# Bias of two chunks in one load, and the order of the first loads: fused attention and MLP on one core

## The chip, the cores and the metric

The kernel runs on one core of a Trainium2 chip. The metric is the device time of one execution in microseconds (us), the median of three runs. KB are 1024 bytes. The core has five engines with a queue of instructions each: TensorE (PE, with its weight loads as PEld), VectorE (DVE), ScalarE (ACT), GpSimd (POOL) and SyncE (SP). SP issues nearly all DMAs of this kernel, in the order of its queue; 16 DMA engines carry them.

## What is computed

Attention with a bias that depends on the distance of two positions, then an MLP over the result (batch 4, 8 heads, 576 positions, head dimension 64):

```python
scores = scale * np.matmul(q, k.transpose(0, 1, 3, 2))
psi_rel = np.log1p(np.abs(rel))
x = (psi_rel / psi_i)[..., None]
h = np.maximum(x @ w1 + b1, 0.0)
bias = h @ w2
scores = scores + bias.transpose(2, 0, 1)[None, :, :, :]
attn = np.exp(scores - max); attn = attn / attn.sum()
out = np.matmul(attn, v)
# then, on x = out as (batch, 576, 512)
u = x + (xt @ U @ V).transpose(0, 2, 1)
result = u + np.maximum(u @ w_ch1, 0.0) @ w_ch2
```

The bias is the same for all four batches; it differs by head.

## The kernel before

**The bias table.** In the first 58 us the kernel computes the bias of all heads, 16 positions at a time (36 blocks), and writes each block to a table in DRAM (`bias_dram`, stored by `bias_out`, L308). From there it comes back as the scores need it. The last five stores of the table hold the last rows, which the last chunks read.

**Pairs, slots, chunks.** Heads are worked in pairs: 16 pairs p (4 batches of 4 head pairs). Only pairs 0 to 3 load bias; pairs 4 to 15 use the same four tiles `bias[hp]` again. The 576 query positions are four chunks c of 128 and a rest of 64 (called c = 4). A pair has nine slots s. Slot 0 works the rest of both heads, slot 1 + 2c the first head of chunk c, slot 2 + 2c its second head. So slots 5 and 6 use chunk 2, and slots 7 and 8 use chunk 3. In a slot (`scores`), TensorE computes a score block of 128x576 into one of two buffers in PSUM, VectorE adds the bias and takes the row minimum of the negated sum (`p<-sc,bias`, L366), ScalarE takes the exponent, and two slots later TensorE transposes the block. Slot 8 ends with a product with v (`av`, out `o`).

**The loads of bias.** `bias_loads(c, hp)` returns the loads of one chunk for one head pair, as closures. A chunk has three: the first head (128 rows of 576 numbers, 288 KB), and the second head in a long part of 512 columns (256 KB) and a short part of 64 columns (32 KB), as its columns stand in the tile in another order. The rest (c = 4) has two loads of 144 KB on 64 partitions each.

**The order of loads.** All of them are issued by SP. A list `loads` holds closures; each slot takes the first two (three in pair 0) and issues them. SP's queue runs ahead of the other engines: a DMA goes out when the ones before it in the queue have gone out and its own waits are over. Each DMA also takes one of eight counters in turn, and SP waits until the DMA that had this counter before has landed; so no more than eight are under way. In the rows of SP's order below these counters are the names DMAHW0 to DMAHW7. A load of bias that reads table rows just stored waits for those stores too.

**Other loads in the same queue.** `load_v` brings v of a pair (320 KB), `load_part` brings q and k of a pair into `raw` in four loads of 304 KB on 64 partitions each, from which GpSimd prepares `hi` and `lo` (`prep_ops`) for the pair after. From slot 0 of pair 2 on, weights of the MLP come too (`wraw`). After the pairs the MLP runs, with a dense TensorE to the end.

Around the change, `bias[p + 1]` of a later pair is asked for in two parts: the rest and chunks 0 and 1 at the pair's start, chunks 2 and 3 (`late`) at its slot 8.

Of the kernel before, what the change touches and what calls it, by code (L numbers as in the profile page):

```python
# [19 lines left out]
B, H, S, D = 4, 8, 576, 64  # L20
# [6 lines left out]
P = 128  # L27
HALF = S // 2
LEFT = S - 4 * P
K0 = 2 * S + LEFT  # L30
QKW = 2 * K0
# [28 lines left out]
def kernel(  # L60
# [14 lines left out]
    nc = tc.nc  # L75
# [52 lines left out]
    bias = {hp: big.tile([P, 9 * S], F32, tag=f"big{hp}", name=f"bias{hp}") for hp in range(2)}  # L128
# [20 lines left out]
    def load_part(p, a, e):  # L149
        b, hp = divmod(p, HP)  # L150
        for lo in (0, D):
            nc.sync.dma_start(out=raw[lo : lo + D, a:e], in_=qk[b, hp, :, a:e])

    def load_v(p):
        b, hp = divmod(p, HP)
        v_t[p] = vpp.tile([P, 640], F32, tag="v", name="v")
        nc.sync.dma_start(out=v_t[p], in_=vp[b, hp])
# [153 lines left out]

    def row(i, h, a, e):
        return bd[i, h * ROW + SHIFT + a : h * ROW + SHIFT + e]

    def bias_loads(c, hp):

        if c < 4:
            i = slice(c * P, (c + 1) * P)
            h, j = 2 * hp, (1 + 2 * c) * S
            parts = [  # L320
                (bias[hp][:, j : j + S], row(i, h, 0, S)),
                (bias[hp][:, j + S + LEFT : j + 2 * S], row(i, h + 1, 0, S - LEFT)),
                (bias[hp][:, j + S : j + S + LEFT], row(i, h + 1, S - LEFT, S)),
            ]
        else:
            i = slice(4 * P, S)
            parts = [(bias[hp][t * LEFT : (t + 1) * LEFT, 0:S], row(i, 2 * hp + t, 0, S)) for t in range(2)]
        return [lambda o=o, i=i: nc.sync.dma_start(out=o, in_=i) for o, i in parts]
# [417 lines left out]
    loads = []  # L746
# [4 lines left out]
    for i in range(len(order) + 2):  # L751
# [4 lines left out]
        if i == len(order) - 1:  # L756
            nc.gpsimd.tensor_scalar(
                out=warm, in0=hids[order[i]][3][:, 0:1], scalar1=1.0, scalar2=0.0, op0=ALU.mult, op1=ALU.add
# [17 lines left out]
    p0.close()  # L776
    psT2 = ctx.enter_context(tc.tile_pool(name="psT2", bufs=2, space=PSUM))
    rot = {"s": [psS], "t": [psT, psT2, psT2]}
    for c, hp in ((4, 1), (0, 1), (3, 0), (1, 1)):
        loads += bias_loads(c, hp)  # L780
    loads += [lambda: load_v(1)] + bias_loads(2, 1)
    loads += [lambda: load_part(2, 0, K0), lambda: load_part(2, K0, QKW)] + bias_loads(3, 1)


    nc.vector.tensor_tensor(out=fold, in0=ident[:, 0 : 2 * RANK], in1=ident[:, 2 * RANK : P], op=ALU.add)
# [1 line left out]
        out=rep[:, 0 : 3 * RANK].rearrange("p (g r) -> p g r", g=3),  # L787
# [5 lines left out]
        out=rep[:, 3 * RANK : P], in0=fold[:, 0:RANK], in1=fold[:, 0:RANK], op=ALU.subtract  # L793
# [28 lines left out]
    for p in range(NP):  # L822
        if p > 0:
            new_pair(p)
        if 0 < p < HP - 1:
            bias[p + 1] = big.tile([P, 9 * S], F32, tag=f"big{p + 1}", name=f"bias{p + 1}")
            loads += [o for c in (4, 0, 1) for o in bias_loads(c, p + 1)]
            late = [o for c in (2, 3) for o in bias_loads(c, p + 1)]
        for s in range(9):
            if s == (1 if p else 0) and p < NP - 1:  # L830
                prep = prep_ops(p + 1)
# [151 lines left out]
    for j in range(3, NB, 2):  # L983
        if j == 3:
            l = utp.tile([P, 4 * LINE + UT], F32R, tag="utl3", name="ut")[:, 4 * LINE :]
            h, l = h3, [(0, l3), (2, l.rearrange("p (k f) -> p k f", k=2))]
        else:
            h = utp.tile([P, KD, 2 * TB], F32R, tag=f"uth{j}", name="ut")
# [15 lines left out]
    def turns(j):  # L1004
        return [lambda a=a, i=i: make_ut(a, i) for a in (j, j + 1) for i in range(TT)] if j < NB else [lambda: None] * 4
# [62 lines left out]
    def store(q, which):  # L1068
        w, to = flat(q, which), (w1_dram, w2_dram)[which][q]
        parts = [slice(o, o + 2 * DM) for o in range(0, w.shape[1], 2 * DM)]  # L1070
        return [lambda c=c: nc.sync.dma_start(out=to[:, c], in_=w[:, c].bitcast(F32)) for c in parts]
# [88 lines left out]
    a = token_sums(5, ([acc[2], acc[3]], [acc[4], acc[5]], [acc[6], acc[7]], [acc[8], acc[9]]), False)  # L1160
# [13 lines left out]
    for u in [(0, j, h) for j in (3, 5, 7) for h in range(2)]:  # L1174
        todo = mlp1(u) + (mlp2(last) if last else [])
        a = turns(u[1] + 2)[2 * u[2] : 2 * u[2] + 2]
# [161 lines left out]
    for q in range(NQ):  # L1338
        final = q == NQ - 1
        new = (w1_sums(q) if q else []) + stream(jobs[q], jobs[q + 1][:2])  # L1340
        late = (store(q - 1, 1) if 0 < q <= 4 else []) + (store(q, 0) if q < 4 else [])
# [3 lines left out]
        segs, c = layer1(q)  # L1345
# [16 lines left out]
    for n, q in enumerate(order2):  # L1362
# [4 lines left out]
        one, c = layer1(q)  # L1367
# [84 lines left out]
```

## Time and profile before

| | us |
|---|---|
| median of three runs | 731.37 |
| lowest and highest run | 730.5, 731.55 |
| the profiled execution | 730.93 |
| its span, from the first to the last instruction | 729.2 |
| TensorE busy in it | 707.6 (97%) |
| VectorE, ScalarE, GpSimd busy | 534.0, 402.6, 265.0 |

The 1.7 us between the span and the execution's time lie around the program. The granted clock of TensorE is 1.00 of its higher level (2.4 GHz) over the whole span. In the rows, L366 is line 366 of the kernel, `out<-in` names tiles, and `<-` in brackets names what ended an engine's idle time.

### The profile page before, as it was taken

Reading aid. Unit: us, or ns where it says so; the run is one execution under the profiler, and the core shown is the slowest. Engines: PE = TensorE matmul, PEld = TensorE weight load, DVE = VectorE, ACT = ScalarE, POOL = GpSimd, SP = SyncE. Lnnn points to the kernel's source line nnn. Section 1 sums busy time; section 2 is a strip of 40 time slices with the busy share of each in tenths; the row PEclk is TensorE's granted clock in tenths of the full one; section 3 lists DMA queues with packets and bytes.
Section 4 is the critical chain, followed back from the end, with each engine's and each line's share of the span. In section 5 each row is a group of like instructions: output and inputs, shape, how many; then the busy total and the mean of one; then the engine's idle time right before and its main releaser. Section 6 shows DMA issues by size and latency. Waiting matters only on the chain.

```text
span 729.2 us, 13122 instructions
## 1 busy us (share of the span) xinstructions
PE 707.6 (97%) x4620; PEld 562.0 (77%) x4620; DVE 534.0 (73%) x1202; ACT 402.6 (55%) x915; POOL 265.0 (36%) x281
## 2 busy tenths in 40 slices
PE   6899999999999999999999999999999999999997
PEld 3446887788777777879787888888787788888886
DVE  7985577788888767665658779989999964655545
ACT  7896777788878768774223235555555421222220
POOL 0004666667756657801141332536346400000000
PEclk9999999999999999999999999999999999999999
DMA  6889997475556556632192613647434674633313
GB/s 195 274 308 311 266 262 197 124 201 144 160 156 174 126 133 174 179 120 87 66 345 107 236 35 119 226 148 262 158 130 159 228 263 168 259 123 129 159 58 116
DMA packets 53874, 129.06 MB, mean 177 GB/s; under 512 B 8881, under 2 KB 12465, under 8 KB 52529
## 3 DMA queue, kind: packets, MB, share of 16 engines
q1 hardware_dynamic: 53568, 127.97, 54.8%
q8 instruction: 37, 0.61, 0.4%
q14 instruction: 29, 0.23, 0.1%
q10 hardware_dynamic: 240, 0.26, 0.1%
HBM read 83.21 MB, written 44.99 MB: 176 GB/s over the span
## 4 chain that ended last, share of the span: by engine, by line
PE 68%; DVE 9%; ACT 8%; DMA 8%; POOL 3%; issue 3%; SPq 1%; POOLq 0%; DVEq 0%; ACTq 0%
PE po L1287 15%; PE sb L1226 12%; PE o L468 9%; PE sc L364 9%; PE tb L432 6%; PE ph L635 5%; PE po L660 4%; DMA bias<-bias_dram 3%; PE bs L291 3%; DMA raw<-in_qk_dram 2%; POOL wy L229 1%; PE ph L1315 1%; DMA u_dram<-acc 1%; DVE acc L1273 1%; ACT ring L271 1%
## 5 line engine op out<-in xcount | busy, mean ns | idle before, releaser
L1273 DVE TENSOR_TENSOR acc<-po,acc 128x512 f32<-128x512 f32 x108 | 74.0, 687 | 50.2 <-PE po L1287 42.8
L385 ACT ACTIVATE p<-p,st 128x576 f32<-128x576 f32 x128 | 100.0, 782 | 13.0 <-DVE st L366 12.5
L366 DVE CUSTOM_DVE_ANT_0 p<-sc,bias 128x576 f32<-128x576 f32 x128 | 95.9, 752 | 14.7 <-PE sc L364 7.1
L364 PE MATMUL sc<-hi 128*128 128x288 f32 x320 | 100.7, 331 | 1.7 <-DVE st L366 1.7
L229 POOL TENSOR_TENSOR wy<-wt,wy 128x256 int32<-128x256 int32 (+1 forms) x68 | 49.9, 733 | 141.5 <-DVE wt L224 124.5
L364 PE MATMUL sc<-lo,hi 128*128 128x288 f32 x320 | 89.2, 295 | 0.0
L468 PE MATMUL o<-pt,v 128*64 128x320 f32 (+1 forms) x640 | 85.4, 411 | 0.1
L432 PE MATMUL tb<-ident,p 128*128 128x128 f32 x512 | 78.2, 275 | 1.3 <-DVE pt L414 0.9
L1287 PE MATMUL po<-wq,hq 128*128 128x512 f32 x288 | 73.4, 391 | 0.4 <-DVE ut L1320 0.4
L364 PEld LDWEIGHTS sc<-hi 128*128 128x128 f32 x320 | 60.4, 189 | 13.0 <-issue 9.0
L432 PEld LDWEIGHTS tb<-ident,p 128*128 128x128 f32 x512 | 59.9, 140 | 10.3 <-issue 7.4
L468 PEld LDWEIGHTS o<-pt,v 128*64 128x64 f32 x640 | 44.3, 136 | 30.2 <-issue 3.2
L412 ACT COPY pt<-tb 128x512 f32<-128x512 f32 x88 | 51.3, 583 | 24.1 <-PE tb L432 24.0
L1287 PEld LDWEIGHTS po<-wq,hq 128*128 128x128 f32 x288 | 53.5, 188 | 12.4 <-DVE ut L1320 0.9
L364 PEld LDWEIGHTS sc<-lo,hi 128*128 128x128 f32 x320 | 60.6, 190 | 0.5
L1226 PE MATMUL sb<-ut,w1q 128*128 128x512 f32 x216 | 55.1, 390 | 0.4 <-ACT acc L1230 0.3
L1226 PE MATMUL sb<-ut,wq 128*128 128x512 f32 x216 | 54.9, 390 | 0.5 <-ACT acc L1230 0.4
L291 PE MATMUL bs<-ring,small_sb 128*32 128x512 f32 (+49 forms) x640 | 44.3, 404 | 9.3 <-ACT ring L271 8.3
L660 PE MATMUL po<-w2q,hh 128*128 128x512 f32 x216 | 52.5, 393 | 0.9 <-DVE acc L663 0.5
L1287 PE MATMUL po<-w2q,ut 128*128 128x512 f32 x180 | 49.1, 389 | 0.0
L635 PE MATMUL ph<-ut,w1q 128*128 128x512 f32 (+1 forms) x240 | 48.2, 351 | 0.5 <-DVE ut L605 0.5
L1226 PEld LDWEIGHTS sb<-ut,w1q 128*128 128x128 f32 x216 | 40.4, 188 | 9.6 <-ACT acc L1230 1.3
(148 smaller groups left out, 1424.8 us busy)
## 6 DMA issues: line engine op xcount, KB each, us to landing
raw<-in_qk_dram SPq DMA_DIRECT2D x56, 304.0 KB, 4.5
wraw<-in_w_ch_dram SPq DMA_DIRECT2D x64, 256.0 KB, 3.2
bias_dram<-ring SPq DMA_DIRECT2D x30, 296.0 KB, 4.3
acc<-u_dram SPq DMA_DIRECT2D x26, 256.0 KB, 4.8
ub_dram<-ut SPq DMA_DIRECT2D x12, 512.0 KB, 5.4
w_dram<-wq SPq DMA_DIRECT2D x12, 512.0 KB, 4.4
ut<-ub_dram SPq DMA_DIRECT2D x12, 512.0 KB, 4.2
v<-in_vp_dram SPq DMA_DIRECT2D x16, 320.0 KB, 3.1
```

What stands on the lines that cost most here:

```text
L229: nc.gpsimd.tensor_tensor(out=st["y"], in0=st["t"], in1=st["y"], op=ALU.add)
L291: mm(bs[T][32 * cg : 32 * cg + 32, o + a : o + e], lhsT=w2_sb, rhs=hid[:, far + left - e : far + left - a][:, ::-1] if a >= left else hid[ ...
L364: mm(ps[:, a, 0:HALF], lhsT=hi[:, q0 : q0 + P], rhs=kk, start=(i == 0), stop=(i == n - 1))
L366: nc.vector.tensor_tensor_reduce(out=halves(dst), in0=ps[:, :, 0:HALF], in1=halves(bias[hp][:, s * S : (s + 1) * S]), scale=-0.125, scalar ...
L385: nc.scalar.activation(out=dst, in_=dst, func=AF.Exp, bias=st[:, s : s + 1], scale=-1.0, accum_out=st[:, 10 + s : 11 + s])
L432: nc.tensor.transpose(bank[:, kb, :], src[:, b0 + kb * P : b0 + (kb + 1) * P], ident)
L468: mm(o[hd * D : (hd + 1) * D, 0:n], lhsT=v[:, vb * D : (vb + 1) * D], rhs=pt[:, pb, :], start=(j == 0), stop=(j == 4),)
L635: mm(st["ps"][:, f, :], lhsT=w, rhs=x, start=(i == 0), stop=(i == 3 * KD - 1))
L660: mm(ps, lhsT=h, rhs=w, start=(m == 0), stop=(m == 3 * nf - 1))
L1226: mm(bank[b], lhsT=w[:, c, r, :], rhs=u[:, r, :], start=first and i == 0, stop=i == 5, skip_group_check=True)
L1273: nc.vector.tensor_tensor(out=a, in0=ps, in1=a, op=ALU.add)
L1287: mm(ps, lhsT=h, rhs=w[:, r, :], start=m == 0, stop=m == 5)
```

## The change

The new helper `bias_two(c, hp)` returns three loads for chunks c and c + 1 of a head pair: both first heads (128x2x576, 576 KB), both long parts (512 KB) and both short parts (64 KB). It takes the place of two calls of `bias_loads` for chunks 0 and 1 and for chunks 2 and 3 of pairs 1, 2 and 3: six times three loads fewer. The chunks of pair 0 stay single. In the first list, chunk 3 of pair 0 now stands ahead of chunk 0 of pair 1, and chunk 2 of pair 1, which stood ahead of the loads of q and k for pair 2, comes with chunk 3 behind them.

```diff
--- before.py
+++ after.py
@@ -311,6 +311,16 @@
 
     def row(i, h, a, e):
         return bd[i, h * ROW + SHIFT + a : h * ROW + SHIFT + e]
+
+    def bias_two(c, hp):
+
+        h, j = 2 * hp, (1 + 2 * c) * S
+        to = bias[hp][:, j : j + 4 * S].rearrange("p (c x) -> p c x", c=2)
+        parts = [
+            (to[:, :, o : o + e - a], row(slice(c * P, (c + 2) * P), i, a, e).rearrange("(c p) x -> p c x", c=2))
+            for o, i, a, e in ((0, h, 0, S), (S + LEFT, h + 1, 0, S - LEFT), (S, h + 1, S - LEFT, S))
+        ]
+        return [lambda o=o, i=i: nc.sync.dma_start(out=o, in_=i) for o, i in parts]
 
     def bias_loads(c, hp):
 
@@ -776,10 +786,8 @@
     p0.close()
     psT2 = ctx.enter_context(tc.tile_pool(name="psT2", bufs=2, space=PSUM))
     rot = {"s": [psS], "t": [psT, psT2, psT2]}
-    for c, hp in ((4, 1), (0, 1), (3, 0), (1, 1)):
-        loads += bias_loads(c, hp)
-    loads += [lambda: load_v(1)] + bias_loads(2, 1)
-    loads += [lambda: load_part(2, 0, K0), lambda: load_part(2, K0, QKW)] + bias_loads(3, 1)
+    loads += bias_loads(4, 1) + bias_loads(3, 0) + bias_two(0, 1) + [lambda: load_v(1)]
+    loads += [lambda: load_part(2, 0, K0), lambda: load_part(2, K0, QKW)] + bias_two(2, 1)
 
 
     nc.vector.tensor_tensor(out=fold, in0=ident[:, 0 : 2 * RANK], in1=ident[:, 2 * RANK : P], op=ALU.add)
@@ -824,8 +832,8 @@
             new_pair(p)
         if 0 < p < HP - 1:
             bias[p + 1] = big.tile([P, 9 * S], F32, tag=f"big{p + 1}", name=f"bias{p + 1}")
-            loads += [o for c in (4, 0, 1) for o in bias_loads(c, p + 1)]
-            late = [o for c in (2, 3) for o in bias_loads(c, p + 1)]
+            loads += bias_loads(4, p + 1) + bias_two(0, p + 1)
+            late = bias_two(2, p + 1)
         for s in range(9):
             if s == (1 if p else 0) and p < NP - 1:
                 prep = prep_ops(p + 1)
```

The instructions of TensorE, VectorE, ScalarE and GpSimd keep their order. On SP it changes. First the place at the end of the bias table, before; `bias_109` is the tile of pair 0, `bias_110` that of pair 1, and the first row is the table's last store:

```order
L308 DMA bias_dram<-e_133 128x592 [waits DMAHW4_49,Activation_49]
L328 DMA bias_110<-bias_dram 64x576 [waits DMAHW5_49]
L328 DMA bias_110<-bias_dram 64x576 [waits DMAHW6_49]
L328 DMA bias_110<-bias_dram 128x576 [waits DMAHW7_49]
L328 DMA bias_110<-bias_dram 128x512 [waits DMAHW0_49]
L328 DMA bias_110<-bias_dram 128x64 [waits DMAHW1_49]
L328 DMA bias_109<-bias_dram 128x576 [waits DMAHW4_49,DMAHW3_49,DMAHW2_49]
L328 DMA bias_109<-bias_dram 128x512
L328 DMA bias_109<-bias_dram 128x64
L328 DMA bias_110<-bias_dram 128x576 [waits DMAHW5_49]
L328 DMA bias_110<-bias_dram 128x512 [waits DMAHW6_49]
L328 DMA bias_110<-bias_dram 128x64 [waits DMAHW7_49]
```

The same place on SP now:

```order
L308 DMA bias_dram<-e_133 128x592 [waits DMAHW4_49,Activation_49]
L338 DMA bias_110<-bias_dram 64x576 [waits DMAHW5_49]
L338 DMA bias_110<-bias_dram 64x576 [waits DMAHW6_49]
L338 DMA bias_109<-bias_dram 128x576 [waits DMAHW4_49,DMAHW3_49,DMAHW7_49,DMAHW2_49,DMAHW0_49]
L338 DMA bias_109<-bias_dram 128x512
L338 DMA bias_109<-bias_dram 128x64 [waits DMAHW1_49]
L323 DMA bias_110<-bias_dram 128x2x576
L323 DMA bias_110<-bias_dram 128x2x512
L323 DMA bias_110<-bias_dram 128x2x64
L157 DMA v<-in_vp_dram 128x640 [waits DMAHW5_49]
L152 DMA raw<-in_qk_dram 64x1216 [waits DMAHW6_49,Pool_49]
L152 DMA raw<-in_qk_dram 64x1216 [waits DMAHW7_49,Pool_49]
```

The load of chunk 3 of pair 0 (`bias_109` 128x576), with its waits for the table's last stores, has moved up past three loads, which come behind it in double form.

The second place on SP is the last bias of all, chunks 2 and 3 of pair 3 (`bias_1144`), before:

```order
L152 DMA raw<-in_qk_dram 64x1216 [waits DMAHW5_49]
L328 DMA bias_1144<-bias_dram 128x576 [waits DMAHW6_49]
L328 DMA bias_1144<-bias_dram 128x512 [waits DMAHW7_49]
L328 DMA bias_1144<-bias_dram 128x64 [waits DMAHW0_49]
L328 DMA bias_1144<-bias_dram 128x576 [waits DMAHW1_49]
L328 DMA bias_1144<-bias_dram 128x512 [waits DMAHW2_49]
L328 DMA bias_1144<-bias_dram 128x64 [waits DMAHW3_49]
L199 DMA wraw<-in_v_dram 128x128 [waits DMAHW4_49,DVE_49,Activation_49]
```

The same place now (the tile is called `bias_1135`):

```order
L152 DMA raw<-in_qk_dram 64x1216 [waits DMAHW6_49]
L323 DMA bias_1135<-bias_dram 128x2x576 [waits DMAHW7_49]
L323 DMA bias_1135<-bias_dram 128x2x512 [waits DMAHW0_49]
L323 DMA bias_1135<-bias_dram 128x2x64 [waits DMAHW1_49]
L199 DMA wraw<-in_v_dram 128x128 [waits DMAHW2_49,DVE_49,Activation_49]
```

Chunk 3's rows now come between chunk 2's first head and the rest of chunk 2.

On VectorE the bias additions of slots 5 to 8 of pair 1 wait as follows, before:

```order
L366 ISA p,st<-sc,bias_110 128x576 [waits DMAHW1_49,PE_49]
L366 ISA st 128x1
L366 ISA p,st<-sc,bias_110 128x576 [waits DMAHW3_49,DMAHW2_49,PE_49]
L366 ISA st 128x1
L414 COPY pt<-ti 128x256 [waits PE_49]
L414 COPY pt<-ti 64x64 x2
L366 ISA p,st<-sc,bias_110 128x576 [waits DMAHW0_49,PE_49,Activation_49]
L366 ISA st 128x1
L414 COPY pt<-tb 128x4x128 [waits PE_49]
L366 ISA p,st<-sc,bias_110 128x576 [waits DMAHW2_49,DMAHW1_49,PE_49]
```

And now:

```order
L376 ISA p,st<-sc,bias_110 128x576 [waits DMAHW2_49,PE_49]
L376 ISA st 128x1
L376 ISA p,st<-sc,bias_110 128x576 [waits DMAHW4_49,DMAHW3_49,PE_49]
L376 ISA st 128x1
L424 COPY pt<-ti 128x256 [waits PE_49]
L424 COPY pt<-ti 64x64 x2
L376 ISA p,st<-sc,bias_110 128x576 [waits PE_49,Activation_49]
L376 ISA st 128x1
L424 COPY pt<-tb 128x4x128 [waits PE_49]
L376 ISA p,st<-sc,bias_110 128x576 [waits PE_49]
```

Slots 5 and 6 wait for the double loads, slots 7 and 8 for no DMA any more.

## Rows read from the trace of the kernel before

**Rows 1.** Stretches: from:to, length, busy us by engine, clock, DMA share, GB/s

```profile
58.00:62.40 4.40, 4.40 (x39) 4.38 (x37) 3.67 (x10) 3.93 (x11) 4.23 (x4) 1.00 1.05 370
62.40:67.00 4.60, 3.71 (x26) 1.77 (x24) 0.13 (x1) 0.16 (x2) 2.45 (x2) 1.00 0.90 280
67.00:111.00 44.00, 43.17 (x336) 35.88 (x337) 29.20 (x85) 34.59 (x88) 24.92 (x24) 1.00 1.04 270
111.00:114.00 3.00, 1.64 (x15) 1.40 (x13) 2.74 (x8) 1.98 (x5) 2.83 (x3) 1.00 1.12 352
114.00:122.50 8.50, 8.50 (x64) 6.49 (x64) 5.99 (x18) 6.81 (x20) 3.74 (x5) 1.00 0.85 183
```

**Rows 2.** Chain that ended last, 50 to 150 us: start us, length us, what

```profile
58.10 4.32 DMA bias_dram<-e
...
63.82 1.64 SPq L328
...
101.76 9.36 DMA bias<-bias_dram
```

**Rows 3.** VectorE's timeline: start, us, line, operation, count, idle before and releaser

```profile
66.87 0.76 DVE L366 CUSTOM_DVE_ANT_0 p<-sc,bias 128x576 f32<-128x576 f32 x1 [4.93 <-DMA bias<-bias_dram]
...
77.41 0.76 DVE L366 CUSTOM_DVE_ANT_0 p<-sc,bias 128x576 f32<-128x576 f32 x1
...
78.81 0.76 DVE L366 CUSTOM_DVE_ANT_0 p<-sc,bias 128x576 f32<-128x576 f32 x1 [0.63 <-PE sc L364]
...
111.24 0.76 DVE L366 CUSTOM_DVE_ANT_0 p<-sc,bias 128x576 f32<-128x576 f32 x1 [1.67 <-DMA bias<-bias_dram]
```

**Rows 4.** TensorE's timeline: the two waits, and slot 8's scores of pairs 1, 3

```profile
67.78 0.37 PE L364 MATMUL sc<-hi 128*128 128x288 f32 x1 [1.67 <-DVE st L366]
...
80.46 0.38 PE L364 MATMUL sc<-hi 128*128 128x288 f32 x1
...
112.67 0.44 PE L449 MATMUL ti<-ident,p 128*128 128x128 f32 x2 [1.36 <-DVE pt L414]
...
113.94 0.38 PE L364 MATMUL sc<-hi 128*128 128x288 f32 x1
```

**Rows 5.** SyncE's issues 58 to 66 us, then each load's size, us to landing

```profile
58.50 3.14 SPq L328 DMA_DIRECT2D bias<-bias_dram  x5
...
62.50 0.32 SPq L328 DMA_DIRECT2D bias<-bias_dram  x1
...
bias<-bias_dram SPq DMA_DIRECT2D x1, 288.0 KB, 4.2
...
65.98 0.43 SPq L328 DMA_DIRECT2D bias<-bias_dram  x1
...
bias<-bias_dram SPq DMA_DIRECT2D x1, 32.0 KB, 3.7
```

**Rows 6.** The same of four later loads; last, a load issued at 120.9 us

```profile
73.08 0.32 SPq L328 DMA_DIRECT2D bias<-bias_dram  x1
...
bias<-bias_dram SPq DMA_DIRECT2D x1, 32.0 KB, 7.5
...
103.02 0.57 SPq L328 DMA_DIRECT2D bias<-bias_dram  x1
...
bias<-bias_dram SPq DMA_DIRECT2D x1, 256.0 KB, 8.8
...
103.62 0.44 SPq L328 DMA_DIRECT2D bias<-bias_dram  x1
...
bias<-bias_dram SPq DMA_DIRECT2D x1, 32.0 KB, 8.4
...
107.66 0.32 SPq L328 DMA_DIRECT2D bias<-bias_dram  x1
...
bias<-bias_dram SPq DMA_DIRECT2D x1, 32.0 KB, 6.0
...
wraw<-in_w_ch_dram SPq DMA_DIRECT2D x1, 256.0 KB, 2.7
```

## The prediction

> **What bounds the kernel now.** I first read the page's busy times: TensorE works 97% of the span, so time can be had only where TensorE stands still, and the view of stretches tells where that is while bias is loaded. TensorE is idle for 0.9 us in 62.4 to 67, 0.8 us in 67 to 111, 1.36 us in 111 to 114, and not at all in the stretches beside these [rows 1]. The DMA column of that view says more: the engines' share is 0.90 or above in every stretch from 58 to 114 and falls after that, with the rate, to 0.85 and 183 GB/s. So up to 114 us one stream of loads runs without a pause, and whoever waits for bias waits for a place in that stream. The chain of waits agrees: it goes through the last store of the bias table (landed at 58.10 + 4.32 = 62.42 us), through SyncE's queue, and then through DMAs up to a bias load that lands at 101.76 + 9.36 = 111.12 us [rows 2].
>
> VectorE's timeline names the two waits [rows 3]. At 66.87 us slot 7 of pair 0 starts after 4.93 us without work: it waited for chunk 3 of pair 0. At 111.24 us slot 5 of pair 3 starts after 1.67 us: it waited for chunk 2 of pair 3. TensorE feels them as 1.67 us before 67.78 and 1.36 us before 112.67 [rows 4], together 3.03 us. In between it is dense. No gain from this change in the attention part can be larger than these 3.03 us.
>
> **The change part by part.** *Bytes.* None is added or taken away; 36 loads become 18. A double load needs 0.32 to 0.6 us of SyncE's time like any other, I take it, since in the rows a 32 KB load and a 288 KB load cost SyncE 0.32 us alike [rows 5, 6]. SyncE's saved issue time lies beside a full stream and is worth nothing there.
>
> *Price of a byte in the stream.* The first-head load of chunk 2 of pair 3 lands at 111.12 us, the last load of chunk 3 at 107.66 + 6.0 = 113.66 us [rows 2, 6]. In between lie 256 + 32 + 288 + 256 + 32 = 864 KB (0.885 MB): 0.885 / 2.54 us = 348 GB/s. At that rate a chunk's first-head load (288 KB) takes 0.85 us and a whole chunk (576 KB) 1.69 us. Other rows bound the first of these: 370 GB/s (58 to 62.4 us) makes it 0.80 us, 270 GB/s (67 to 111 us) 1.09 us [rows 1].
>
> *Chunk 3 of pair 0 ahead of chunk 0 of pair 1.* Chunk 3 cannot be asked for before 62.42 us, when the last store has landed; its first load starts at 62.50 us before [rows 5] and will not start earlier after. But SyncE's queue is in order. Before, five loads are issued from 58.50 us on ahead of it (two rest loads, three loads of chunk 0) [rows 5], so 576 KB fill the time until the store lands. After, only the two rest loads stand there, and behind the waiting load are queued chunks 0 and 1 of pair 1, v of pair 1 and q/k of pair 2. The gain: chunk 3's first load meets an empty stream. Before, it needed 4.2 us; a load of 256 KB into an idle stream needs 2.7 us [rows 5, 6]. It lands between 65.2 (2.7 us) and 66.7 us; I take 65.5 us, close to the idle row, since the two small rest loads are nearly done. Slot 7 then starts 1.3 us earlier, and TensorE's 1.67 us before 67.78 shrink to about 0.4 us. The price: chunk 0 must now follow. Before, the last load of chunk 1 landed at 65.98 + 3.7 = 69.7 us [rows 5]. After, 256 + 32 KB of chunk 3 and two chunks, 1440 KB (1.475 MB, 4.24 us), land behind chunk 3's first load: at 65.5 + 4.24 = 69.7 us, with ends 69.4 and 70.9 us. So the stream stands where it stood: 0 us, from -0.3 to +1.2 us. Before also lost time here: one issue of SyncE took 1.64 us [rows 2], while the DMA share was 0.90.
>
> *Chunk 2 of pair 1 behind q/k of pair 2.* Chunks 2 and 3 of pair 1 now land together, ending where chunk 3 ended: 73.08 + 7.5 = 80.6 us [rows 6]. The double load with both first heads ends the other two (512 + 64 KB, 1.69 us) earlier, at 78.9 us. Slot 5 of pair 1 used its chunk at 77.41, slot 6 at 78.81 us [rows 3], so here stand two new waits of 1.5 and 1.8 us, more than the 1.3 us won in pair 0. Slot 8's scores start on TensorE at 80.46 us [rows 4] and need the score buffer that slot 6 leaves at 80.6 + 0.1 + 0.76 = 81.5 us: pair 1 ends about 1.0 us later. This costs nothing as long as VectorE's 1.67 us at slot 5 of pair 3 cover it; without that cover it would be 1.0 us. q/k of pair 2 come 1.7 us earlier, but TensorE didn't wait for them.
>
> *Chunk 2 of pair 3, the last wait.* By 111 us the same bytes have gone through the stream, so it stands at 0 again. But slot 5 no longer waits for 288 KB of chunk 2: the load holds chunk 3's first head too, and the program has one wait for the whole of it. It lands 0.85 us later (0.80 to 1.09), at 111.97 us. Slot 5 and TensorE's restart at 112.67 us move by 0.85 us. Slot 6 needs the rest, landed at 113.66 us: it ends at 113.66 + 0.12 + 0.76 = 114.54 us, and slot 8's scores on TensorE, at 113.94 us before [rows 4], then stand at 114.79 us, so this second wait is hidden. After 114 us the rate falls and TensorE sets the time, so the shift stays to the end.
>
> No run here shows a double load. The Trainium skill speaks against it ("DMA: Bandwidth & Descriptors", section "Why a DMA increments its semaphore by 16 and not by 1"): only the full count means that all has landed, so chunk 2's user pays for chunk 3's half. Without that rule the sum would be 0 in place of +0.85 us.
>
> *Sum.* 0 (stream) + 0.85 (merging at the last wait) + 0 (pairs 0 and 1, covered) = +0.85 us. The profiled execution took 730.93 us and would take 731.8. The median of the runs is 731.37 us, 0.4 us above it, so I forecast 731.37 + 0.85 = 732.2 us.
>
> **The rivals.** A difference under 0.2% (1.46 us) can hardly be told from no change here; faster means below 729.9, slower above 732.8 us.
>
> *Slower: the gap before the store's landing is paid in full.* If chunk 3's first load still needs 4.2 us, the stream stands 1.2 us later from 70 us on and has no pause in which to catch up, so that the last wait moves by 1.2 + 0.85 = 2.05 us: 733.4 us. It decides from a landing of chunk 3's first load later than 66.1 us (0.6 us behind my 65.5). For it: after the two rest loads nothing is under way, and the share of 0.90 shows that the stream can run dry at this place. Against it: 2.7 us on an idle stream.
>
> *Faster: larger loads go through the stream more quickly.* The 32 KB load lands 0.2 us behind the 256 KB one (103.02 + 8.8 = 111.8; 103.62 + 8.4 = 112.0) [rows 6], where 348 GB/s make 0.09 us. If the 0.1 us is a cost per load, 18 loads fewer save 1.8 us by 111 us, less 0.85: 730.4 us; if loads of eight in flight also hold the engines back, at most TensorE's 3.03 us go: 728.3 us. The skill's same page (section "Rules for kernel authors") says to coalesce small transfers; its section "Why small descriptors are slow" lays the cost on short rows instead, which this change keeps. By the second the saving is 0. Against it: a share of 1.04 from 67 to 111 us leaves no visible gaps between loads.
>
> *It reaches nothing.* If the stream gains the 0.85 us back before 111 us (SyncE's 1.64 us issue [rows 2] now has two double loads under way ahead of it), the last wait ends where it ended: 731.4 us.
>
> **How the numbers follow.** Forecast 0.45, at 731.5 to 732.8 us; slower rival 0.25; faster rival 0.22, of which 0.16 below 729.9 us; nothing 0.08. Slower takes 0.25 and 0.02 of the forecast's upper edge: 0.27. Faster 0.16. The rest, 0.57, is within 0.2%. The range leaves out the best of the faster rival (about 0.12) and the worst of the slower one (0.06): 729.8 to 733.9 us.
>
> **What would show it.** Right: SyncE issues only two loads between 58.5 and 62.4 us; slot 7 of pair 0 starts at about 65.6 us; slots 5 and 6 of pair 1 wait for bias; slot 5 of pair 3 starts at about 112.1 us, and TensorE's gap there is longer than 1.36 us. Wrong: a DMA share or rate from 67 to 111 us clearly above 1.04 and 270 GB/s, or a landing of pair 3's chunk 2 before 111 us, makes the faster rival true; a landing after 113 us the slower one. If slot 5 of pair 3 moves by 0.85 us and the end doesn't, the later part of the kernel takes shifts up, which I have left out.

## The result, and the profile after

The changed kernel takes 735.2 us (median; 734.0 to 736.9) against 731.4 us before: a ratio of 1.0057, 95% interval 1.0037 to 1.0077. A later series of twelve runs (e12 below) gave 735.35 against 731.32 us, 1.0053 (1.0031 to 1.0074). The change costs 3.9 to 4.0 us, and the time lies 1.3 us above the upper end of the predicted range. The profiled execution of after is one of its longer ones: 736.9 us, 6.0 us above the profiled 730.93 us of before, so its rows show somewhat more than the median. And one trace is one execution: at slot 6 of pair 0, ahead of all that the versions below move, their traces stand between -0.28 and +1.35 us against before, so a shift under about 1 us in a single trace is not read as an effect.

The view of stretches of after, with the columns of [rows 1] (from:to, length, busy us of TensorE, its weight loads, VectorE, ScalarE, GpSimd, then clock, DMA share, GB/s):

```profile
58.00:62.40 4.40, 4.40 (x39) 4.40 (x38) 3.67 (x10) 3.93 (x10) 4.23 (x4) 1.00 1.02 378
62.40:67.00 4.60, 4.56 (x33) 2.63 (x32) 1.37 (x3) 1.12 (x4) 2.69 (x2) 1.00 0.73 223
67.00:111.00 44.00, 39.71 (x277) 31.47 (x276) 23.28 (x69) 29.38 (x76) 19.16 (x17) 0.92 1.03 265
111.00:114.00 3.00, 3.00 (x25) 1.88 (x26) 2.70 (x9) 2.02 (x6) 1.89 (x4) 1.00 1.04 298
76.00:81.70 5.70, 3.38 (x29) 3.15 (x28) 1.70 (x6) 3.12 (x9) 4.83 (x4) 1.00 1.06 270
81.70:88.50 6.80, 6.19 (x26) 4.33 (x26) 3.83 (x11) 4.39 (x11) 3.45 (x3) 0.50 1.07 286
```

Three things differ from [rows 1]. From 62.4 to 67 us TensorE is now busy throughout (4.56 us against 3.71), but the DMA engines move 223 GB/s at a share of 0.73, where they moved 280 at 0.90. From 67 to 111 us TensorE loses 3.5 us of work at a DMA share that has hardly moved (1.03 against 1.04). And the granted clock falls to 0.50 (the level of 1.2 GHz) from 81.7 to 88.5 us; before, it was 1.00 everywhere. Ahead of the fall TensorE worked 3.38 of 5.70 us.

VectorE's timeline of after, at the slots that wait for bias (start, us, line, operation, idle before and releaser; L376 is L366 of before):

```profile
65.47 0.76 DVE L376 CUSTOM_DVE_ANT_0 p<-sc,bias 128x576 f32<-128x576 f32 x1 [3.30 <-DMA bias<-bias_dram]
...
80.56 0.76 DVE L376 CUSTOM_DVE_ANT_0 p<-sc,bias 128x576 f32<-128x576 f32 x1 [3.63 <-DMA bias<-bias_dram]
83.19 0.76 DVE L376 CUSTOM_DVE_ANT_0 p<-sc,bias 128x576 f32<-128x576 f32 x1 [1.86 <-DMA bias<-bias_dram]
...
116.90 0.76 DVE L376 CUSTOM_DVE_ANT_0 p<-sc,bias 128x576 f32<-128x576 f32 x1 [0.47 <-DMA bias<-bias_dram]
```

These are slot 7 of pair 0, slots 5 and 6 of pair 1, and slot 5 of pair 3. Against [rows 3] they stand at -1.40, +3.15, +4.38 and +5.66 us. So the first wait became shorter, as it was meant to, and everything was lost again, and more, at chunk 2 of pair 1. TensorE's timeline of after shows that this wait reaches it:

```profile
68.51 0.40 PE L374 MATMUL sc<-hi 128*128 128x288 f32 x1 [0.40 <-DVE st L376]
...
81.38 0.40 PE L374 MATMUL sc<-hi 128*128 128x288 f32 x1 [2.32 <-DVE st L376]
...
84.01 0.61 PE L374 MATMUL sc<-hi 128*128 128x288 f32 x1 [0.61 <-DVE st L376]
```

The 1.67 us ahead of 67.78 [rows 4] are down to 0.40, but 2.32 and 0.61 us are new. From slot 8 of pair 1 (+4.29 us) to slot 0 of pair 2 (91.82 against 86.18 us, +5.64) another 1.35 us go: that is in the stretch with the half clock. A third loss is slot 6 of pair 2 (102.35 against 94.97 us, +7.38; it was +5.65 at slot 5). This slot starts 0.5 us behind the landing of the double load of both short parts (last line of the next view), as it does in e4, e10 and e12 below. Some is taken back at slot 5 of pair 3 (from +6.86 us at slot 4 to +5.66), and from pair 4 on the shift is +6.0 us.

SyncE's issues of six loads of after, each with its size and the us to its landing:

```profile
62.42 0.33 SPq L338 DMA_DIRECT2D bias<-bias_dram  x1
...
bias<-bias_dram SPq DMA_DIRECT2D x1, 288.0 KB, 2.9
...
64.73 1.46 SPq L323 DMA_DIRECT2D bias<-bias_dram  x1
...
bias<-bias_dram SPq DMA_DIRECT2D x1, 64.0 KB, 7.6
...
69.81 0.58 SPq L323 DMA_DIRECT2D bias<-bias_dram  x1
...
bias<-bias_dram SPq DMA_DIRECT2D x1, 576.0 KB, 10.6
...
71.91 0.37 SPq L323 DMA_DIRECT2D bias<-bias_dram  x1
...
bias<-bias_dram SPq DMA_DIRECT2D x1, 512.0 KB, 10.8
...
107.48 0.38 SPq L323 DMA_DIRECT2D bias<-bias_dram  x1
...
bias<-bias_dram SPq DMA_DIRECT2D x1, 576.0 KB, 9.3
...
91.02 0.38 SPq L323 DMA_DIRECT2D bias<-bias_dram  x1
...
bias<-bias_dram SPq DMA_DIRECT2D x1, 64.0 KB, 10.8
```

Chunk 3 of pair 0 (first row) lands 2.9 us after its issue, at 65.3 us. The last load of chunks 0 and 1 of pair 1 lands at 64.73 + 7.6 = 72.3 us, where before it landed at 69.7 [rows 5]. Of chunks 2 and 3 of pair 1, both first heads land at 80.4 us and both long parts at 82.7 us, where the last load of chunk 3 landed at 80.6 us before [rows 6]. The first heads of chunks 2 and 3 of pair 3 land at 116.8 us (chunk 2's before at 111.12 [rows 2]). The last load shown, of both short parts of chunks 2 and 3 of pair 2, lands at 101.8 us.

### The profile page after: what moved, and what is told of

Read it like the earlier page. It is cut to its first block, busy times and chain, and to the rows that moved or that the text cites. A ratio compares the mean times of both kernels' runs of the same rounds, so it can differ in the third digit from the quotient of the medians.

```text
span 735.1 us, 13100 instructions
## 1 busy us (share of the span) xinstructions
PE 712.2 (97%) x4620; PEld 564.1 (77%) x4620; DVE 534.7 (73%) x1202; ACT 403.4 (55%) x915; POOL 265.2 (36%) x281
## 4 chain that ended last, share of the span: by engine, by line
PE 67%; DVE 9%; DMA 8%; ACT 8%; POOL 4%; issue 3%; SPq 1%; POOLq 0%; DVEq 0%; ACTq 0%
PE po L1295 15%; PE sb L1234 11%; PE o L478 9%; PE sc L374 9%; PE tb L442 6%; PE ph L645 5%; DMA bias<-bias_dram 4%; PE po L670 4%; PE bs L291 3%; POOL wy L229 2%; DVE acc L1281 1%; ACT ring L271 1%; PE ph L1323 1%; DMA raw<-in_qk_dram 1%; DMA u_dram<-acc 1%
## 5 line engine op out<-in xcount | busy, mean ns | idle before, releaser
L376 DVE CUSTOM_DVE_ANT_0 p<-sc,bias 128x576 f32<-128x576 f32 x128 | 95.9, 752 | 20.0 <-DMA bias<-bias_dram 9.9
L1238 ACT COPY acc<-sb 128x512 f32<-128x512 f32 x48 | 27.9, 584 | 36.1 <-PE sb L1234 36.0
```

The source lines that it names most:

```text
L376: nc.vector.tensor_tensor_reduce(out=halves(dst), in0=ps[:, :, 0:HALF], in1=halves(bias[hp][:, s * S : (s + 1) * S]), scale=-0.125, scalar ...
```

## The experiments

Each kernel ran twelve times beside runs of the kernel before on the same chip; e1 to e4, e5 to e8 and e9 to e12 were run together.

| run | what differs | median us (before) | ratio, 95% interval |
|---|---|---|---|
| e1 | chunk 3 of pair 0 first, single loads | 733.9 (731.45) | 1.0042 (1.0026 to 1.0058) |
| e2 | chunk 2 of pair 1 behind q/k, single | 731.09 (731.45) | 0.9995 (0.9982 to 1.0008) |
| e3 | both moves, single | 734.01 (731.45) | 1.0039 (1.0023 to 1.0055) |
| e4 | double loads without the two moves | 733.59 (731.45) | 1.0031 (1.0013 to 1.0049) |
| e5 | double loads for chunks 0, 1 only | 732.59 (731.30) | 1.0016 (1.0000 to 1.0031) |
| e6 | double loads for chunks 2, 3 only | 732.91 (731.30) | 1.0024 (1.0007 to 1.0041) |
| e7 | e1 with the empty time filled | 731.66 (731.30) | 1.0012 (0.9996 to 1.0028) |
| e8 | before, late chunks ahead of q/k | 733.96 (731.30) | 1.0033 (1.0014 to 1.0052) |
| e9 | e4 with 4-byte loads between | 732.79 (731.32) | 1.0018 (0.9999 to 1.0037) |
| e10 | the change, filled as e7, 4-byte loads as e9 | 732.64 (731.32) | 1.0010 (0.9987 to 1.0033) |
| e11 | before with 4-byte loads between | 733.81 (731.32) | 1.0026 (1.0006 to 1.0047) |
| e12 | the change again | 735.35 (731.32) | 1.0053 (1.0031 to 1.0074) |

### The parts of the change, one by one: e1 to e4

Chunk 3 of pair 0 ahead of chunk 0 of pair 1, alone:

```diff
-    for c, hp in ((4, 1), (0, 1), (3, 0), (1, 1)):
+    for c, hp in ((4, 1), (3, 0), (0, 1), (1, 1)):
```

> All loads single; only chunk 3 of pair 0 stands ahead of chunk 0 of pair 1. If the order makes the change slow (576 KB leave the gap before the last store lands and the stream never catches up), this alone costs 0.5 to 1.5 us against before, and slot 5 of pair 3 starts 0.5 to 1.5 us later than 111.24 us. If the double loads make it slow, the time is within 0.4 us of before.

It costs 2.45 us, more than both expectations. The view of stretches of e1 (columns as above):

```profile
62.40:67.00 4.60, 3.90 (x27) 2.20 (x28) 1.35 (x4) 0.55 (x1) 2.20 (x2) 1.00 0.66 194
87.70:91.10 3.40, 3.40 (x16) 3.37 (x16) 1.24 (x4) 1.32 (x3) 0.00 (x0) 0.50 1.00 245
67.00:111.00 44.00, 40.95 (x302) 32.71 (x301) 26.11 (x78) 31.08 (x80) 21.04 (x21) 0.96 1.02 270
```

The stretch behind the store's landing moves (280 - 194) GB/s x 4.6 us = 0.40 MB less than before, at the 348 GB/s of the prediction 1.1 us of stream. VectorE's timeline of e1 has a new wait for bias at slot 7 of pair 1 (+1.92 us):

```profile
82.31 0.76 DVE L366 CUSTOM_DVE_ANT_0 p<-sc,bias 128x576 f32<-128x576 f32 x1 [3.19 <-DMA bias<-bias_dram]
```

But it isn't this wait that TensorE feels. TensorE's waits of e1 from 60 to 125 us (what waited, for what, us in total, times, longest):

```profile
PE sc L364 <- POOL lo L178: 2.1, 2, 1.2
PE sc L364 <- POOL hi L170: 0.9, 1, 0.9
PE sc L364 <- DVE st L366: 0.7, 1, 0.7
```

The last is the shortened wait in pair 0. The other 3.0 us, from 83.6 to 87.5 us, are waits for `hi` and `lo` of pair 2, which GpSimd prepares from q and k. GpSimd begins when the second of the four q/k loads has landed. This load in e1 (issue, then size and us to landing), and in the chain of before:

```profile
70.25 1.12 SPq L152 DMA_DIRECT2D raw<-in_qk_dram  x1
...
raw<-in_qk_dram SPq DMA_DIRECT2D x1, 304.0 KB, 8.5
```

```profile
68.98 6.52 DMA raw<-in_qk_dram
```

It lands at 78.7 us in place of 75.5, and GpSimd starts 0.2 us behind it in both (78.89 and 75.68 us). So the time lost in the stream came due at q and k of pair 2, with the 3.4 us at the clock of 0.50 behind it, and the shift is +3.82 us at slot 2 of pair 2. At slot 5 of pair 3, which doesn't wait for bias in e1, 1.73 us are taken back; +2.29 us stay.

Chunk 2 of pair 1 behind q/k of pair 2, alone:

```diff
-    loads += [lambda: load_v(1)] + bias_loads(2, 1)
-    loads += [lambda: load_part(2, 0, K0), lambda: load_part(2, K0, QKW)] + bias_loads(3, 1)
+    loads += [lambda: load_v(1)]
+    loads += [lambda: load_part(2, 0, K0), lambda: load_part(2, K0, QKW)] + bias_loads(2, 1) + bias_loads(3, 1)
```

> All loads single; only chunk 2 of pair 1 stands behind q and k of pair 2. Order theory: slots 5 and 6 of pair 1 wait 1 to 3 us for bias, and part of it reaches the end, +0.5 to +1.5 us, since TensorE's pause there lowers its clock as it did in the changed kernel. Double-load theory: pair 1's wait is covered by the 1.67 us of pair 3, and the time is within 0.4 us of before.

It costs nothing that can be measured, and slots 5 and 6 of pair 1 don't wait for bias. Both moves together, with single loads:

> The changed kernel's order of loads in full, but every load single. Order theory: the whole of the change's 3.9 us, +3 to +4 us. Double-load theory: at most +1 us, and the last of the 16 DMA engines lands no more than 3 us behind the first, as before.

They cost what the first costs alone, 2.56 us: less than the order theory expected, more than the other. The profiled execution took 731.25 us, 2.8 us below that median, so its trace does not show this cost. Double loads without the two moves:

```diff
-    for c, hp in ((4, 1), (0, 1), (3, 0), (1, 1)):
-        loads += bias_loads(c, hp)
-    loads += [lambda: load_v(1)] + bias_loads(2, 1)
-    loads += [lambda: load_part(2, 0, K0), lambda: load_part(2, K0, QKW)] + bias_loads(3, 1)
+    loads += bias_loads(4, 1) + bias_two(0, 1) + bias_loads(3, 0) + [lambda: load_v(1)]
+    loads += bias_two(2, 1) + [lambda: load_part(2, 0, K0), lambda: load_part(2, K0, QKW)]
...
-            loads += [o for c in (4, 0, 1) for o in bias_loads(c, p + 1)]
-            late = [o for c in (2, 3) for o in bias_loads(c, p + 1)]
+            loads += bias_loads(4, p + 1) + bias_two(0, p + 1)
+            late = bias_two(2, p + 1)
```

> Double loads for pairs 1 to 3 as in the changed kernel, but in the old order: chunks 0 and 1 of pair 1 ahead of chunk 3 of pair 0, chunks 2 and 3 of pair 1 ahead of q and k of pair 2. Order theory: at most +0.85 us, the price of merging in the prediction. Double-load theory: +2.5 to +4 us, with waits for bias in pairs 2 and 3 and loads that land 6 us and more behind the stream's pace.

This isn't quite the order of before, since merging moves loads as well. Chunk 1 of pair 1 now stands ahead of chunk 3 of pair 0 (here, in e5 and in e9), and chunk 3 of pair 1 ahead of q and k of pair 2 (here, in e6 and in e9); before, both stood behind. The change itself has neither.

They cost 2.14 us, with a granted clock of 1.00 over the whole profiled execution. VectorE's timeline of e4 at slots 5 and 6 of pair 3, and the double load of both second heads with its landing:

```profile
112.66 0.76 DVE L376 CUSTOM_DVE_ANT_0 p<-sc,bias 128x576 f32<-128x576 f32 x1 [0.38 <-PE tb L442]
115.57 0.76 DVE L376 CUSTOM_DVE_ANT_0 p<-sc,bias 128x576 f32<-128x576 f32 x1 [1.54 <-DMA bias<-bias_dram]
```

```profile
102.19 0.47 SPq L323 DMA_DIRECT2D bias<-bias_dram  x1
...
bias<-bias_dram SPq DMA_DIRECT2D x1, 512.0 KB, 12.5
```

Slot 5 comes 1.42 us later, slot 6 3.04 us: the second heads land at 114.7 us and their last 64 KB at 115.4 us, 1.8 us later than the last of the six single loads that these three replace (113.66 us before [rows 6]). A merged wait alone can't do that: the bytes themselves are later.

The two shifts of order show as well. From issue to landing, the first load of chunk 3 of pair 0 needs 5.5 us in e4, 6.6 in e5 and 6.3 in e9, where chunks 0 and 1 of pair 1 (1152 KB) stand ahead of it, and 3.8 to 4.4 us in before, e2, e6, e8 and e11, where it is chunk 0 alone (576 KB). TensorE's wait for it in e4 (before: 1.67 us [rows 4]):

```profile
69.02 0.37 PE L374 MATMUL sc<-hi 128*128 128x288 f32 x1 [2.84 <-DVE st L376]
```

And q and k of pair 2 land later: GpSimd starts on them at 77.96 us (before 75.68). The next q/k load waits for GpSimd's last step on them and is issued at 86.58 us (before 84.31), and with it wait the loads behind it in SyncE's queue. The stretches of e4, then of before:

```profile
82.00:87.00 5.00, 5.00 (x36) 3.04 (x35) 1.99 (x6) 3.31 (x9) 4.38 (x4) 1.00 0.68 178
87.00:92.00 5.00, 5.00 (x45) 4.59 (x44) 3.57 (x11) 3.64 (x9) 1.93 (x3) 1.00 0.82 202
```

```profile
82.00:87.00 5.00, 5.00 (x38) 3.51 (x39) 1.59 (x6) 2.54 (x7) 2.29 (x2) 1.00 1.07 297
87.00:92.00 5.00, 5.00 (x43) 4.24 (x42) 3.02 (x10) 4.03 (x11) 3.34 (x4) 1.00 1.01 249
```

So for 10 us the stream of e4 ran partly empty. The 2.14 us are the price of doubling together with these two shifts.

### Where the cost of doubling lies: e5 and e6

The same, for chunks 0 and 1 only (e5: `late` and chunks 2, 3 of pair 1 single) or for chunks 2 and 3 only (e6).

> Double loads for chunks 0 and 1 of pairs 1 to 3 alone; chunks 2 and 3 single, in the old order. Theory 'a double load is paid by the one who waits for its first half': nobody waits for chunks 0 and 1 of pairs 2 and 3, so the time stays at 731.4 us (within 0.7 us) and slot 5 of pair 3 starts within 0.5 us of 111.24 us. Theory 'more bytes under way make the stream itself late': the cost is shared by both kinds of double loads, so about half of the 2.1 us that doubling cost in full: 732.5 us, and chunk 2 of pair 3, though single, lands about 1 us later.

> Double loads for chunks 2 and 3 of pairs 1 to 3 alone; chunks 0 and 1 single, as before. Theory 'paid by the one who waits for its first half': all of the 2.1 us that doubling cost in full stands here: 733.5 us, slot 5 of pair 3 starts 0.9 to 1.5 us later and slot 6 waits too. Theory 'more bytes under way make the stream late': about half: 732.5 us.

Both cost about as much, 1.3 and 1.6 us. In e5 chunks 2 and 3 are single, and yet chunk 2 of pair 3, for which slot 5 waits as it did before, comes later. The load, and VectorE's timeline, of e5:

```profile
102.78 0.34 SPq L338 DMA_DIRECT2D bias<-bias_dram  x1
...
bias<-bias_dram SPq DMA_DIRECT2D x1, 288.0 KB, 10.2
```

```profile
113.12 0.76 DVE L376 CUSTOM_DVE_ANT_0 p<-sc,bias 128x576 f32<-128x576 f32 x1 [1.10 <-DMA bias<-bias_dram]
```

A single load of 288 KB lands at 113.0 us, 1.9 us later than before. What TensorE feels in e5 begins earlier, though. Its two waits:

```profile
69.50 0.37 PE L374 MATMUL sc<-hi 128*128 128x288 f32 x1 [3.55 <-DVE st L376]
...
114.54 0.44 PE L459 MATMUL ti<-ident,p 128*128 128x128 f32 x2 [0.79 <-DVE pt L424]
```

Before they were 1.67 and 1.36 us [rows 4]. The cost arises at chunk 3 of pair 0, with the order; the late landing of chunk 2 of pair 3 only keeps the wait there from taking all of it back (+2.44 us at slot 4, +1.88 at slot 5). In e6, 1.4 us of TensorE's waits are for GpSimd's `lo` of pair 2, so again for q and k.

The trace has 16 completion events for each load, and each counts as landed with the last. The Trainium skill ("DMA: Bandwidth & Descriptors", section "Why a DMA increments its semaphore by 16 and not by 1") says that these are the marks of up to 16 engines that finish independently. The events of the load with the first head of chunk 2 of pair 3, and the mean time from the first to the last event over all loads issued from 67 to 110 us (4-byte loads left out), worked out from the traces:

```
kernel    size     first       9th       last       mean spread, us
before    288 KB   109.79     110.45     111.12        1.92
e5        288 KB   109.87     110.39     112.99        3.24
e4        576 KB   110.66     110.82     112.53        2.50
e6        576 KB   110.95     111.35     112.73        2.16
e1        288 KB   111.50     112.01     113.22        2.27
e8        288 KB   107.78     108.06     109.47        2.34
e9        576 KB   111.21     111.58     112.86        1.47
e11       288 KB   112.16     112.50     112.79        1.63
after     576 KB   112.51     113.20     116.77        4.29
e12       576 KB   112.92     114.38     116.64        4.06
```

In e5 the first and the middle engine are where they were before; the last one is 1.9 us later. So here it isn't the stream as a whole that is late: its engines have drifted apart, and the landing goes by the slowest. In after, the last engine is 3.6 us behind the middle one, and at the load that slot 6 of pair 2 waits for 4.7 us (97.14 and 101.84 us). The mean has to be read with care: single loads in other orders (e1, e2, e3, e7, e8) spread by 1.81 to 2.34 us. After, e12 and e5 stand clear of that, e4 hardly, and e6 not at all, though it costs as much as e5.

How many bytes are under way is set by the program: a load takes the completion counter of the load eight places ahead of it, and SyncE issues it when that one has landed (in before, the load issued at 75.52 us stood eight places behind a q/k load that landed at 75.51 us). Eight places filled with double loads hold up to twice the bytes. That the quick engines then run further ahead, before SyncE waits for the slow one, is an argument; e9 and e10 test it.

### Fewer bytes under way, and the empty time filled: e7, e9 to e12

In e7, v of pair 1 and a quarter of q/k of pair 2, which need no bias table, stand ahead of chunk 3 of pair 0:

```diff
-    for c, hp in ((4, 1), (0, 1), (3, 0), (1, 1)):
+    loads += bias_loads(4, 1) + [lambda: load_v(1)] + [lambda: load_part(2, 0, K0, (0,))]
+    for c, hp in ((3, 0), (0, 1), (1, 1), (2, 1)):
         loads += bias_loads(c, hp)
-    loads += [lambda: load_v(1)] + bias_loads(2, 1)
-    loads += [lambda: load_part(2, 0, K0), lambda: load_part(2, K0, QKW)] + bias_loads(3, 1)
+    loads += [lambda: load_part(2, 0, K0, (D,)), lambda: load_part(2, K0, QKW)] + bias_loads(3, 1)
```

> Chunk 3 of pair 0 ahead of chunk 0 of pair 1, as in the change, with single loads; but ahead of it, in the time before the last table store lands, stand v of pair 1 and a quarter of q/k of pair 2, which need no table: 624 KB in place of chunk 0's 576 KB. Theory 'the loss is the empty stretch before the store lands': the stretch 62.4 to 67 us has a DMA share of 0.9 or more again and the time goes back to 731.4 us (within 0.8 us), slot 7 of pair 0 at 66.5 to 67.5 us. Theory 'chunks of pair 1 have become late by the order itself': 733.5 to 734 us as with chunk 3 first alone.

Of e1's 2.45 us, 0.4 are left, and these are within the measurement. The stretches of e7:

```profile
62.40:67.00 4.60, 4.46 (x32) 2.50 (x30) 0.27 (x2) 0.91 (x3) 3.12 (x3) 1.00 1.00 255
67.00:111.00 44.00, 41.38 (x321) 34.14 (x322) 28.98 (x84) 32.87 (x84) 23.13 (x23) 1.00 1.04 272
```

The share of 0.66 is 1.00 again. One part of the expectation failed: slot 7 of pair 0 starts at 68.65 us, later than before, not at 66.5 to 67.5, so filling the time gives up the gain that the move was made for. The wait at slot 5 of pair 3 takes up 0.83 us of that 1.78 us.

In e9 and e10 a load of 4 bytes into a tile of its own follows each double load, so that every second counter holds almost nothing; e10 is the change with both e7's list and these loads.

```diff
+    def with_mark(o, i):
+        n = next(mark_at)
+        nc.sync.dma_start(out=o, in_=i)
+        nc.sync.dma_start(out=mark[:, n : n + 1], in_=vp[0, 0, 0:1, n : n + 1])
...
-        return [lambda o=o, i=i: nc.sync.dma_start(out=o, in_=i) for o, i in parts]
+        return [lambda o=o, i=i: with_mark(o, i) for o, i in parts]
```

> Double loads in the old order (the kernel of the run with doubling alone), with a load of 4 bytes behind each double load. In the trace of before the issue of a load waits until the load eight places ahead of it has landed, so the 4-byte loads take every second of eight places and as many bytes are under way as with single loads. Theory 'too many bytes under way: the DMA engines drift apart and a load has landed only when the last engine is done': the engines' spread at 95 to 113 us goes back from 2 to 3 us to the 1.2 to 2 us of before, and only the merged wait at slot 5 of pair 3 stays: 731.4 to 732.3 us. Rival 'the size of a load and the merged wait cost the time': 733.6 us as with doubling alone, spread unchanged.

> The change with both suspected costs mended: chunk 3 of pair 0 stays ahead of chunk 0 of pair 1, but v of pair 1 and a quarter of q/k of pair 2 stand ahead of it and fill the time before the last table store lands; and a 4-byte load stands behind each double load. If the empty stretch and the bytes under way account for the change's cost: 731.4 to 732.5 us. If something else of the change costs time: 733.5 us or more.

> The kernel before with a load of 4 bytes behind the first-head load of each chunk of pairs 1 to 3: fewer bytes under way than before, nothing else changed. Theory 'bytes under way': the engines' spread at the loads of pair 3's chunk 2 falls below the 1.33 us of before, chunk 2 lands up to 0.5 us earlier, 730.9 us, at best 730.4. Rival 'before has already few enough under way': 731.4 us, or slower by SyncE's extra issues, 0.3 to 0.6 us each, if these leave the stream short.

> The changed kernel as it is, beside the other three on the same chip. By its earlier runs 735.2 us, 734 to 737 us. Where its profile shows a granted clock of 1.000, the sum of the two parts run apart (2.5 us for chunk 3 first, 2.1 us for doubling) would make 736.0 us; the smaller 735.2 us would mean that the waits they make cover one another in part.

The spread went as expected: from 2.50 us in e4 to 1.47 in e9, and 1.97 in e10 against 4.06 in the change beside it. So fewer bytes under way do bring the engines together. The time of e9, 732.8 us, lies between the two expectations and can't be told from e4's. In its trace TensorE has one long wait up to 122 us, 4.13 us for chunk 3 of pair 0, so what is left in e9 begins with the order too. e10 is 2.7 us faster than the change on the same chip and can't be told from before: filling the empty time and holding fewer bytes under way, together, take away about two thirds of the change's cost; the 1.3 us that are left are within the measurement.

e11 sets the limit of this. It has a smaller spread than before (1.63 us) and is 2.5 us slower. Its stretch:

```profile
67.00:111.00 44.00, 42.29 (x322) 33.70 (x319) 28.54 (x82) 32.78 (x83) 22.72 (x23) 1.00 0.98 262
```

The DMA share is 0.98 in place of 1.04: the engines stay together and run short of work. Whether the fewer bytes under way do that, or the time of SyncE's extra issues, e11 doesn't tell. Either way a 4-byte load has a price too, and e9's time contains it.

### Asking earlier for the last waits: e8

```diff
-            if s == 8 and 0 < p < HP - 1:
-                loads += late
             n = 2 if p else 3
+            if s == 7 and 0 < p < HP - 1:
+                loads += late
+                n = len(loads)
```

> The kernel before, but chunks 2 and 3 of pairs 2 and 3 are asked for at slot 7 of the pair ahead, in front of the second half of the q/k loads of the pair after the next. Theory 'the last wait for bias, slot 5 of pair 3, is paid in full to the end': chunk 2 of pair 3 has 608 KB less ahead of it, at 348 GB/s 1.8 us, lands near 109.3 us, the 1.67 us of VectorE and the 1.36 us of TensorE there go, and the time is 730.0 us. Rival 'the wait goes over to q/k of pair 4': its second half lands 1.7 us later, at about 112.2 us; if the end doesn't move, 731.4 us, or more if POOL's work on q/k is late for pair 4.

The wait at slot 5 of pair 3 is gone (110.70 us in place of 111.24), and the kernel is 2.7 us slower. GpSimd's timeline of e8, and VectorE at slot 0 of pair 4:

```profile
116.33 1.32 POOL L170 TENSOR_SCALAR hi<-raw 128x1216 fp32r<-128x1216 f32 x1 [3.57 <-DMA raw<-in_qk_dram]
```

```profile
122.09 0.76 DVE L366 CUSTOM_DVE_ANT_0 praw<-sc,bias 128x576 f32<-128x576 f32 x1 [5.50 <-PE sc L364]
```

The second half of q/k of pair 4 has become the late load; slot 0 of pair 4 starts 2.45 us later. The rival was right. As in e1, what was pushed over its due time is a load of q and k. None of these versions beats before.

## Why the prediction was wrong

**What bounds the kernel: read in part.** The stream of loads up to 114 us and TensorE's gaps were read rightly. But the chain that ended last [rows 2] was said to go from SyncE's queue through DMAs alone. Between them it has these pieces (before, start us, length us, what):

```profile
68.98 6.52 DMA raw<-in_qk_dram
...
75.68 1.22 POOL hi L170
...
81.32 2.98 POOL lo L178 x2
84.31 6.67 DMA raw<-in_qk_dram
```

From 75.68 to 84.30 us it is GpSimd's work on q and k of pair 2, and the q/k load of 84.31 us waits for that. The prediction followed bias alone and left this path out; TensorE's new waits of e1, and in part those of e6 and e8, lie on it.

**Chunk 3 of pair 0 ahead, 0 us (-0.3 to +1.2): wrong, 2.45 us alone.** The gain was sized well: landing at 65.3 us (65.5 predicted), slot 7 at 65.47 (65.6). The failed step is "1440 KB land behind it at 69.7 us": they landed at 72.3 us, 2.6 us behind before. It took 348 GB/s, a rate read where eight loads queue, for a stream that starts from empty; measured were 223 GB/s from 62.4 to 67 us, 0.26 MB less than before (0.75 us at 348 GB/s, an estimate). That is the smaller part: the middle engine (9th event) of the last of these loads is only 0.9 us later than before (69.51 against 68.64 us), and the last engine stands 2.8 us behind it, where it stood 1.0 us behind. The rival that the gap is paid in full named the first half of this, but its condition was wrong: chunk 3's first load landed before 66.1 us, and the gap was paid all the same, by the loads behind it. That its price (733.4 us) is close to e1 (733.9) is luck: it let the last wait for bias move, and in e1 that wait is gone and the time went at q and k of pair 2.

**"Covered by 1.67 us at slot 5 of pair 3": right as a rule, far too small.** Slots 5 and 6 of pair 1 were to start 1.5 and 1.8 us later and started 3.15 and 4.38 us later. Their double load of first heads landed at 80.4 us in place of 78.9, while its middle engine was done at 78.51. Where slot 5 of pair 3 no longer waits for bias, the cover is there in full (1.73 us in e1, 1.74 in e3); where it still waits, less is left of it (0.83 us in e7, 1.20 in after, from +6.86 us at slot 4 to +5.66).

**The merged wait, +0.85 us: mechanism right, size wrong.** Slot 5 of pair 3 moved 1.42 us in e4 and 1.62 us in e6, each time 0.1 us behind the landing of the merged load. "This second wait is hidden" failed: it went by chunk 3's old landing at 113.66 us, while the double load landed at 114.7 to 115.4, and slot 6 was the late one (+3.04 us). The prediction let a larger load cost only its bytes. That the engines drift apart, and that loads which were not doubled pay for this as well (e5), stood in none of its cases. How much of doubling's 2.1 us is drift, how much the merged wait and how much the two shifts of order in e4, the runs don't settle.

**Larger loads go through more quickly: wrong.** From 67 to 111 us the share is 1.03 and the rate 265 GB/s, against 1.04 and 270. The Trainium skill ("DMA: Bandwidth & Descriptors", section "Rules for kernel authors") asks for loads of 1 MiB or more for the most bandwidth; here 512 and 576 KB in place of 256 and 288 KB gave no more of it, and a later landing.

**Chunk 2 of pair 1 behind q/k, 0 us: right** (e2, -0.4 us, within the measurement).

**Left out: the clock.** A wait of TensorE was counted as its length. In after it is followed by 6.8 us at half the clock, in which another 1.35 us go by slot 0 of pair 2.

The parts, 2.45 + 2.14 - 0.36 = 4.2 us, come near the 3.9 to 4.0 us of the change, but that is no proof: e4 holds two shifts of order that the change doesn't have, and e1 drew on the cover at slot 5 of pair 3, which can be used only once.

## What to carry to other kernels

Where one in-order stream of loads sets the time, what stands ahead of a load that must wait for a store matters more than what it delays: fill that time with loads that need nothing, or leave it filled. Before merging loads, ask not only who waits for the merged half but how many bytes the completion counters then let run, and look at the last engine's completion, not at the stream's rate. Merging two loads also moves one of them past what stood between them. A gain at the first wait of a full stream is worth nothing unless the later due times in it have room; list them all before moving one, also those of loads that another engine (here GpSimd, with q and k) must work on first.

## What was not expected of the hardware

The DMA engines of one queue drift apart, by 1.9 us on average between the first and the last at a load in before and by 4.3 us in after; which engines fall behind, and why, stays open. And a TensorE that had stood for 2.32 us was granted a clock of 0.50 for the 6.8 us that followed, while working 6.19 of them; in e1 it was 3.4 us. The traces of e3, e5, e8, e9 and e10 have a fall of 3.4 us too. In e4 a wait of 2.84 us ahead of 69.02 us was followed by no fall, so the length of one wait alone doesn't tell it; what decides is open here.
